# Stationary columns 16 bytes apart in place of 8, for the second weight of four of sixteen blocks

## The chip, the cores and the metric

The kernel runs on one core of a Trainium2 chip. The metric is device time in microseconds (us) of one execution. TensorE runs two kinds of instruction that matter here: a weight load (LDWEIGHTS, rows of "PEld"), which takes a stationary matrix of 128 rows and up to 128 columns from SBUF into the array, and a matmul (rows of "PE"), which streams a moving matrix of up to 512 columns through it. The load of the next matmul can run beside the matmul before it.

## The reference

```python
def _attn_ref(q, k, v):                     # q, k, v: 8 batches, 8 heads, 576 positions, 64 wide
    scores = scale * np.matmul(q, k.transpose(0, 1, 3, 2))
    bias = slopes[:, None, None] * (-np.abs(rel).astype(np.float32))[None, :, :]
    mask = (rel >= 0) & (rel < window)      # window 128
    ...                                     # softmax
    return np.matmul(attn, v).astype(np.float32)

def _moe_ref(x, w_in, w_out):               # x: 4608 tokens x 512; w_in 512x2048; w_out 2048x512
    h = np.maximum(x @ w_in, 0.0)
    return (h * h @ w_out).astype(np.float32)
```

The attention's output, one row for each token, is the input x of the two large products.

## The kernel before, in words

The 4608 tokens are worked in 9 chunks of 512 (c = 0 to 8), the 2048 hidden features in 16 blocks of 128 (f = 0 to 15). All weights are loaded once and stay in SBUF. Float32 accuracy is kept by splitting each operand in a high and a low part of the type fp32r (wh and wl of a weight, hh and hl of the hidden values) and adding three products: high by high, high by low, low by high.

For each chunk and block, `gemm1(c, f)` (matmuls in line 183) makes a 128x512 piece of the hidden layer from 4 contraction blocks of 3 products each, so 12 pairs of a weight load and a matmul; ScalarE and VectorE square and split it. `gemm2(c, f)` (matmuls in line 215) multiplies this piece by the second weight: 4 output blocks of 128 columns (m = 0 to 3), 3 products each, again 12 pairs, which add up in four PSUM banks over all f. From chunk 1 on the order on TensorE is written out in the main loop: `gemm1(n)`, `gemm2(n - 2)`, `gemm1(n + 1)`, `gemm2(n - 1)`, and so on. After every fourth `gemm1` the main loop puts the attention of a pair of heads in between: `values` of one pair (line 336) and `scores` of the next (line 388), together called a visit below. The block of `gemm2` that stands directly behind a visit has f = 1, 5, 9 or 13:

```python
                q, part = divmod(t - FIRST, 8)
```

with FIRST = 39, t = 2n or 2n + 1: part is 0 at t = 39, 47, 55, ..., so behind `gemm1` of n = 19, 23, 27, ..., and `gemm2` of n - 2 follows. Chunk 0 has an order of its own, planned ahead in `start`, in which visits of another kind stand between the blocks. Behind the last visit, in chunk 8, 35 pieces of 12 pairs follow each other without a visit.

In SBUF a weight block w[f] has for each partition two matrices (first and second weight) of 512 columns, and each column is 8 bytes: the low part and beside it the high part (the source is float64, whose two words `convert` rewrites in place). So a weight load of 128 columns reads 128 values that lie 8 bytes apart:

```python
        wh, wl = self.w[f][:, 1, :, 1], self.w[f][:, 1, :, 0]
```

Of the kernel before, what the change touches and what calls it, by code (L numbers as in the profile page):

```python
# [21 lines left out]
DM, DF = 512, 2048  # L22
NF = DF // 128
# [12 lines left out]
GO = 20  # L36
SOON = (("z", 7),)
FIRST = 39
CASTS = (0, 2, 15,)
COPIES = (3,)  # L40
SQUARES = (6,)
# [14 lines left out]
def slope(h):  # L56
    return 2.0 ** (-8.0 * (h + 1) / H)


class Kern:  # L60
# [91 lines left out]
    def weights_load(self, f):  # L152
        nc = self.nc
        at = lambda name, dt: nc.alloc_sbuf_tensor_at(f"{name}{f}", [128, 2, 512, 2], dt, offset=self.arena + f * 8192).ap()
        self.raw[f], self.w[f] = at("raw", I32), at("w", F32R)
        for i, d in enumerate((self.w1d, self.w2d.rearrange("(f p) d -> f p d", p=128))):
            nc.sync.dma_start(self.raw[f][:, i].rearrange("p d t -> p (d t)"), d[f].bitcast(I32))

    def convert(self, f):
# [8 lines left out]
        yield  # L168
        (nc.gpsimd.tensor_copy if f in CASTS else nc.scalar.copy)(wh, flo)
        yield  # L170
        nc.vector.tensor_tensor(wl, flo, wh.bitcast(F32), op=ALU.subtract)

    def gemm1(self, c, f):
        nc = self.nc
        xs = [self.x[c, p] for p in range(NP)]
        g = self.g1.tile([128, 512], F32, name="g")
        wh, wl = self.w[f][:, 0, :, 1], self.w[f][:, 0, :, 0]
        i = 0  # L180
        for cc in range(NCC):
            for w, part in ((wh, 0), (wh, 1), (wl, 0)):
                nc.tensor.matmul(  # L183
                    g, w[:, cc * 128 : cc * 128 + 128], xs[cc][:, part], start=i == 0, stop=i == 11
                )
                i += 1
                if (c, f, i) == (0, 0, 9):
                    yield
        yield
        r = self.hp.tile([128, 512], F32, name="r", bufs=1)  # L190
        hh = self.hp.tile([128, 512], F32R, name="hh")
        hl = self.hp.tile([128, 512], F32R, name="hl")
        self.h[c, f] = hh, hl
        with self.tc.high_priority(offset=100):
            nc.scalar.activation(r, g, AF.Relu)  # L195
        yield
        if c or f in SQUARES:
            nc.vector.tensor_tensor(r, r, r, op=ALU.mult)  # L198
        else:
            nc.scalar.activation(r, r, AF.Square)  # L200
        yield
        nc.scalar.copy(hh, r)  # L202
        yield
        nc.vector.tensor_tensor(hl, r, hh.bitcast(F32), op=ALU.subtract)  # L204

    def gemm2(self, c, f):
        nc = self.nc
        hh, hl = self.h.pop((c, f))
        if f == 0:
            self.acc = self.start_banks if c == 0 else [self.ac.tile([128, 512], F32, name="acc") for _ in range(4)]  # L210
        wh, wl = self.w[f][:, 1, :, 1], self.w[f][:, 1, :, 0]
        for m in range(4):
            ms = slice(m * 128, m * 128 + 128)
            for i, (w, h) in enumerate(((wh, hh), (wh, hl), (wl, hh))):
                nc.tensor.matmul(  # L215
                    self.acc[m], w[:, ms], h, start=(f == 0 and i == 0), stop=(f == NF - 1 and i == 2)
                )
            if f == NF - 1:
                o = self.op.tile([128, 512], F32, name="o")
                out = self.outd[m * 128 : m * 128 + 128, 512 * c : 512 * c + 512]  # L220
                if c == NCH - 1 and m == 3:
                    nc.scalar.copy(o[:, 0:256], self.acc[m][:, 0:256])
                    nc.vector.tensor_copy(o[:, 256:512], self.acc[m][:, 256:512])  # L223
                    nc.sync.dma_start(out[:, 0:256], o[:, 0:256])
                    nc.scalar.dma_start(out[:, 256:512], o[:, 256:512])
                    continue
                (nc.scalar.copy if m % 2 else nc.vector.tensor_copy)(o, self.acc[m])
                nc.sync.dma_start(out, o)
# [375 lines left out]
def start(K):  # L604
# [81 lines left out]
    for f in range(NF):  # L686
        d, last = CONV(f), ("w", f)
        g = K.convert(f)
        for i, (engine, us) in enumerate(CONVERT):
            if i == 3 and f in CASTS:  # L690
                engine, us = "Pool", 1.5
# [25 lines left out]
def tile_attn_moe(ctx: ExitStack, tc: tile.TileContext, *aps):  # L717
    K = Kern(ctx, tc, *aps)
    K.const()
    with tc.manual_schedule(engines={ENGINES["PE"]}):  # L720
# [4 lines left out]
        for n in range(NF, NF * NCH + 2):  # L725
            for t in (2 * n, 2 * n + 1):
                q, part = divmod(t - FIRST, 8)
                q += 9
# [17 lines left out]
def _consts():  # L746
    r = np.arange(128)
    own, h = r % 64, (r // 64)[:, None]
    cst = np.zeros((128, CST), np.float32)
    cst[:, 0:128] = np.eye(128)  # L750
    keep = own[:, None] >= np.arange(64)[None, :]
    cst[:, 128:192] = np.where(h == 0, keep, ~keep).astype(np.int32).view(np.float32)
    cst[:, 192:256] = NEG
    rel = r[:, None] - r[None, :]
    rel = np.where(rel >= 0, rel, rel + 128)
    for a in range(H):
        cst[:, 256 + 128 * a : 384 + 128 * a] = -rel * (8 * slope(a))
    later = r[:, None] < r[None, :]
    near = [cst[:, 256 + 128 * a : 384 + 128 * a] for a in range(H)]
    return np.concatenate([cst] + [np.where(late, t, np.float32(NEG)) for t in near for late in (later, ~later)], axis=1)  # L760


def _arrays(q, k, v, moe_w_in, moe_w_out):
    a = np.ascontiguousarray
    pairs = lambda x: x.transpose(1, 3, 0, 2).reshape(NP, 128, B * S)
    halo = lambda x: np.concatenate([np.zeros((NP, 128, 128), np.float32), x], axis=2)
    qt, kt = pairs(q), halo(pairs(k))
    qkd = np.stack([np.concatenate([
        qt[:, :, 512 * c : 512 * c + 256], kt[:, :, 512 * c : 512 * c + 640], qt[:, :, 512 * c + 256 : 512 * c + 512],
    ], axis=2) for c in range(NCH)])  # L770
    vt = np.zeros((NP, 1 + B * S // 128, 128, 128), np.float32)
    vt[:, 1:] = v.reshape(B, NP, 2, S, D).transpose(1, 0, 3, 2, 4).reshape(NP, B * S // 128, 128, 128)
    vd = np.stack([vt[:, 4 * c : 4 * c + 5].transpose(0, 2, 1, 3).reshape(NP, 128, 640) for c in range(NCH)])
    w1d = a(moe_w_in.reshape(NCC, 128, NF, 128).transpose(2, 1, 0, 3).reshape(NF, 128, NCC * 128))
    return [a(qkd), a(vd), w1d.view(np.int64), a(moe_w_out).view(np.int64), _consts()]


# [16 lines left out]
```

## Time and profile before

| | us |
|---|---|
| median of 3 runs | 963.27 (962.99 to 963.32) |
| time of the profiled execution | 963.21 |
| its span, first to last instruction | 961.3 |
| TensorE busy with matmuls | 953.0 (99%) |
| TensorE busy with weight loads | 790.6 (82%) |
| VectorE busy | 485.8 (51%) |
| ScalarE busy | 415.3 (43%) |
| GpSimd busy | 206.1 (21%) |

The busy time of matmuls counts each from its beginning to its modelled end; they overlap, so that the distance from one beginning to the next, and not a row's mean, says how fast they follow each other. In the chain of work that ended last, a piece such as "x12" is one `gemm1` or `gemm2`, and its length over 12 is that distance.

### The profile page before, as it was taken

Reading aid. Unit: us, or ns where it says so; the run is one execution under the profiler, and the core shown is the slowest. Engines: PE = TensorE matmul, PEld = TensorE weight load, DVE = VectorE, ACT = ScalarE, POOL = GpSimd, SP = SyncE. Lnnn points to the kernel's source line nnn. Section 1 sums busy time; section 2 is a strip of 40 time slices with the busy share of each in tenths; the row PEclk is TensorE's granted clock in tenths of the full one; section 3 lists DMA queues with packets and bytes.
Section 4 is the critical chain, followed back from the end, with each engine's and each line's share of the span. In section 5 each row is a group of like instructions: output and inputs, shape, how many; then the busy total and the mean of one; then the engine's idle time right before and its main releaser. Section 6 shows DMA issues by size and latency. Waiting matters only on the chain.

```text
span 961.3 us, 17337 instructions
## 1 busy us (share of the span) xinstructions
PE 953.0 (99%) x6392; PEld 790.6 (82%) x6392; DVE 485.8 (51%) x1335; ACT 415.3 (43%) x1107; POOL 206.1 (21%) x254
## 2 busy tenths in 40 slices
PE   9899999999999999999999999999999999999998
PEld 5688888888888888888888888888888888888886
DVE  6998864444545454544444444445445444433222
ACT  7898743333434443434443343334334343322221
POOL 4123331222222122122222222222221221120000
PEclk9999999999999999999999999999999999999999
DMA  9974423222432333222333332224332221111001
GB/s 348 404 268 151 145 72 113 83 72 64 118 83 83 83 95 105 83 67 76 118 81 83 82 109 66 81 83 127 83 83 72 66 89 42 45 44 44 1 1 44
DMA packets 73028, 95.11 MB, mean 99 GB/s; under 512 B 8048, under 2 KB 42224, under 8 KB 72944
## 3 DMA queue, kind: packets, MB, share of 16 engines
q1 hardware_dynamic: 72512, 93.49, 31.9%
q8 instruction: 50, 0.82, 0.4%
q10 hardware_dynamic: 432, 0.52, 0.2%
q14 instruction: 34, 0.28, 0.1%
HBM read 67.76 MB, written 26.21 MB: 98 GB/s over the span
## 4 chain that ended last, share of the span: by engine, by line
PE 95%; DMA 4%; ACT 0%; DVE 0%; issue 0%; SPq 0%
PE acc L215 43%; PE g L183 42%; PE at L336 6%; PE s L388 3%; PE g L388 2%; DMA raw<-in_dram 2%; DMA wide<-in_dram 1%; DMA qk<-in_dram 1%; PE at L388 0%; ACT raw L163 0%; DVE raw L165 0%; ACT t L422 0%; ACT t L415 0%; DVE o L223 0%; DVE xu L302 0%
## 5 line engine op out<-in xcount | busy, mean ns | idle before, releaser
L183 PE MATMUL g<-xu,w 128*128 128x512 f32 x1728 | 426.2, 395 | 0.8 <-issue 0.8
L183 PEld LDWEIGHTS g<-xu,w 128*128 128x128 f32 x1728 | 336.6, 195 | 66.3 <-issue 1.5
L215 PE MATMUL acc<-hh,w 128*128 128x512 f32 x1152 | 387.8, 398 | 0.0
L215 PEld LDWEIGHTS acc<-hh,w 128*128 128x128 f32 x1152 | 224.9, 195 | 45.3 <-issue 0.7
L215 PE MATMUL acc<-hl,w 128*128 128x512 f32 x576 | 227.3, 395 | 0.0
L198 DVE TENSOR_TENSOR r<-r 128x512 f32<-128x512 f32 x129 | 91.9, 712 | 263.6 <-ACT r L195 263.6
L195 ACT ACTIVATE r<-g 128x512 f32<-128x512 f32 x144 | 85.7, 595 | 314.6 <-PE g L183 311.0
L324 POOL TENSOR_SCALAR_AFFINE_SELECT pp<-pp 128x512 f32<-128x512 f32 x128 | 106.2, 830 | 242.7 <-DMA way<-pp 138.6
L204 DVE TENSOR_TENSOR hl<-r,hh 128x512 fp32r<-128x512 f32 x144 | 106.9, 743 | 68.8 <-ACT hh L202 68.3
L202 ACT CAST hh<-r 128x512 fp32r<-128x512 f32 x144 | 89.2, 620 | 109.2 <-DVE r L198 108.4
L215 PEld LDWEIGHTS acc<-hl,w 128*128 128x128 f32 x576 | 112.5, 195 | 20.5
L260 POOL TENSOR_TENSOR t<-t,nm 128x512 f32<-128x512 f32 x64 | 74.3, 1162 | 237.1 <-DVE nm L257 225.1
L249 ACT ACTIVATE t<-t,nm 128x128 f32<-128x128 f32 x256 | 99.5, 390 | 42.9 <-DVE nm L242 42.9
L434 DVE COPY_PREDICATED t<-cst,s 64x256 f32<-64x256 int32 x100 | 44.4, 444 | 41.0 <-ACT t L422 22.3
L336 PEld LDWEIGHTS at<-pp,v 128*64 128x64 f32 x1024 | 55.2, 137 | 11.4 <-issue 11.4
L336 PE MATMUL at<-pp,v 128*64 128x128 f32 x1024 | 63.0, 276 | 0.0
L242 DVE CUSTOM_DVE_ANT_0 t<-t,cst 128x128 f32<-128x128 f32 x256 | 58.5, 292 | 1.0
L311 DVE STREAM_TRANSPOSE pp<-t 128x512 f32<-128x512 f32 x64 | 45.3, 709 | 22.8 <-POOL t L260 19.9
L388 PE MATMUL s<-qk 64*64 64x64 f32 (+2 forms) x1168 | 47.5, 251 | 0.9 <-ACT raw L163 0.9
L249 ACT ACTIVATION_READ_ACCUMULATOR t<-t,nm 128x1 f32 x256 | 47.9, 187 | 0.0
L388 PEld LDWEIGHTS s<-qk 64*64 64x64 f32 x1168 | 43.0, 133 | 1.1 <-ACT raw L163 1.1
L424 POOL MEMSET t<- 64x128 f32 (+1 forms) x44 | 10.0, 228 | 146.2 <-PE g L388 137.3
(65 smaller groups left out, 476.1 us busy)
## 6 DMA issues: line engine op xcount, KB each, us to landing
raw<-in_dram SPq DMA_DIRECT2D x32, 512.0 KB, 8.7
way<-pp SPq DMA_DIRECT2D x256, 64.0 KB, 1.8
pp<-way SPq DMA_DIRECT2D x64, 256.0 KB, 2.7
qk<-in_dram SPq DMA_DIRECT2D x32, 320.0 KB, 3.7
v<-in_dram SPq DMA_DIRECT2D x32, 320.0 KB, 2.9
qk<-in_dram SPq DMA_DIRECT2D x38, 256.0 KB, 4.3
out_dram<-o SPq DMA_DIRECT2D x35, 256.0 KB, 3.0
v<-in_dram SPq DMA_DIRECT2D x3, 256.0 KB, 5.1
```

Source lines behind the costliest of these rows:

```text
L183: nc.tensor.matmul(g, w[:, cc * 128 : cc * 128 + 128], xs[cc][:, part], start=i == 0, stop=i == 11)
L195: nc.scalar.activation(r, g, AF.Relu)
L198: nc.vector.tensor_tensor(r, r, r, op=ALU.mult)
L202: nc.scalar.copy(hh, r)
L204: nc.vector.tensor_tensor(hl, r, hh.bitcast(F32), op=ALU.subtract)
L215: nc.tensor.matmul(self.acc[m], w[:, ms], h, start=(f == 0 and i == 0), stop=(f == NF - 1 and i == 2))
L242: self.nc.vector.tensor_tensor_reduce(self.t[:, m], self.t[:, m], self.K.nrel(2 * self.p + m // 2), -0.125, BIG, ALU.add, ALU.min, self.nm ...
L249: self.nc.scalar.activation(self.t[:, m], self.t[:, m], AF.Exp, bias=nm[:, m : m + 1], scale=-1.0, accum_out=nm[:, 4 + m : 5 + m],)
L260: self.nc.gpsimd.tensor_tensor(self.t, self.t, self.nm[:, 8:12].unsqueeze(2).to_broadcast([128, 4, 128]), op=ALU.mult)
L324: nc.gpsimd.affine_select(to, self.own, pattern=[[-32 * sign, 4], [0, 4], [-sign, 32]], compare_op=op, fill=0.0, base=0, channel_multiplie ...
L336: self.nc.tensor.matmul(self.X[r, o : o + 128].rearrange("p (a c) -> p a c", a=4), v[:, 2 * sg + k, r], src[:, :, 2 * j + i], start=sg == ...
L388: mm = nc.tensor.matmul(to, qk[r, q0 : q0 + 64], qk[r, k0 : k0 + 64 * n], start=True, stop=True, skip_group_check=True,)
```

## The change

In the second weight of blocks f = 1, 5, 9 and 13 the host stores the columns in another order: within each 256 columns (two output blocks of 128), a column of the one block and a column of the other stand in turn. Output block b of such a weight is then read with every second column, so its 128 values lie 16 bytes apart. All other weights are read as before, 8 bytes apart. Bytes moved, instructions and their order on every engine are the same; only the access pattern of the stationary operand differs, in 4 of 32 weight matrices, or 432 of 3456 weight loads of the two products (36 pieces of 12).

```diff
+APART = lambda i, f, b: i == 1 and f % 4 == 1
...
+    def block(self, i, f, b):
+
+        w = self.w[f][:, i]
+        if APART(i, f, b):
+            w = w.rearrange("p (n j o) t -> p n o j t", n=2, o=2)[:, b // 2, b % 2]
+        else:
+            w = w[:, 128 * b : 128 * b + 128]
+        return w[..., 0], w[..., 1]
...
-        wh, wl = self.w[f][:, 1, :, 1], self.w[f][:, 1, :, 0]
         for m in range(4):
-            ms = slice(m * 128, m * 128 + 128)
+            wl, wh = self.block(1, f, m)
             for i, (w, h) in enumerate(((wh, hh), (wh, hl), (wl, hh))):
                 nc.tensor.matmul(
-                    self.acc[m], w[:, ms], h, start=(f == 0 and i == 0), stop=(f == NF - 1 and i == 2)
+                    self.acc[m], w, h, start=(f == 0 and i == 0), stop=(f == NF - 1 and i == 2)
                 )
...
+    w2d = moe_w_out.reshape(NF, 128, DM).copy()
+    for i, w in enumerate((w1d, w2d)):
+        for f in range(NF):
+            for n in range(2):
+                if APART(i, f, 2 * n):
+                    x = w[f, :, 256 * n : 256 * n + 256]
+                    x[:] = x.reshape(128, 2, 128).transpose(0, 2, 1).reshape(128, 256).copy()
```

## Rows read from the trace of the kernel before

**Rows 1.** The page: span, busy time of TensorE, its granted clock, the chain by engine.

```profile
span 961.3 us, 17337 instructions
...
PE 953.0 (99%) x6392; PEld 790.6 (82%) x6392; DVE 485.8 (51%) x1335; ACT 415.3 (43%) x1107; POOL 206.1 (21%) x254
...
PEclk9999999999999999999999999999999999999999
...
PE 95%; DMA 4%; ACT 0%; DVE 0%; issue 0%; SPq 0%
```

**Rows 2.** The chain in order of time, window 343 to 369: start, length, what.

```profile
343.15 2.97 PE acc L215 x12
346.12 2.76 PE g L183 x12
...
365.44 1.90 PE at L336 x32
```

**Rows 3.** The same, window 549 to 575.

```profile
548.85 3.02 PE acc L215 x12
551.87 2.80 PE g L183 x12
...
571.47 1.90 PE at L336 x32
```

**Rows 4.** The chain's longest pieces over the whole span, the first and the last two behind visits.

```profile
135.84 3.00 PE acc L215 x12
...
834.76 3.02 PE acc L215 x12
859.28 3.01 PE acc L215 x12
```

**Rows 5.** The chain, window 859 to 960, behind the last visit.

```profile
862.29 2.80 PE g L183 x12
...
946.29 2.80 PE g L183 x12
```

**Rows 6.** Timeline of matmuls behind a visit: start, length, what.

```profile
368.52 0.27 PE L388 MATMUL g<-qk 64*64 64x128 f32 x1
368.72 0.51 PE L215 MATMUL acc<-hh,w 128*128 128x512 f32 x1
369.07 0.40 PE L215 MATMUL acc<-hl,w 128*128 128x512 f32 x1
369.30 0.62 PE L215 MATMUL acc<-hh,w 128*128 128x512 f32 x2
```

**Rows 7.** Timeline of weight loads at the same place.

```profile
368.72 0.19 PEld L215 LDWEIGHTS acc<-hh,w 128*128 128x128 f32 x1
368.83 0.20 PEld L215 LDWEIGHTS acc<-hl,w 128*128 128x128 f32 x1
369.07 0.43 PEld L215 LDWEIGHTS acc<-hh,w 128*128 128x128 f32 x2
```

**Rows 8.** Weight loads by line and form: count, busy us, mean ns, idle before.

```profile
L183 PEld LDWEIGHTS g<-xu,w 128*128 128x128 f32 x1728 | 336.6, 195 | 66.3 <-issue 1.5 <-ACT r L195 0.5
L215 PEld LDWEIGHTS acc<-hh,w 128*128 128x128 f32 x1152 | 224.9, 195 | 45.3 <-issue 0.7
...
L388 PEld LDWEIGHTS s<-qk 64*64 64x64 f32 x1168 | 43.0, 133 | 1.1 <-ACT raw L163 1.1
...
L503 PEld LDWEIGHTS acc<-qk__202 64*128 64x128 f32 x8 | 0.7, 186 | 0.2 <-issue 0.2
```

**Rows 9.** The page's DMA issues: the weights' transfer.

```profile
raw<-in_dram SPq DMA_DIRECT2D x32, 512.0 KB, 8.7
```

More of the change, by code (lines that the diff above doesn't have):

```diff
@@ L155, in weights_load @@
         self.raw[f], self.w[f] = at("raw", I32), at("w", F32R)
-        for i, d in enumerate((self.w1d, self.w2d.rearrange("(f p) d -> f p d", p=128))):
+        for i, d in enumerate((self.w1d, self.w2d)):
             nc.sync.dma_start(self.raw[f][:, i].rearrange("p d t -> p (d t)"), d[f].bitcast(I32))
@@ L178, in gemm1 @@
         g = self.g1.tile([128, 512], F32, name="g")
-        wh, wl = self.w[f][:, 0, :, 1], self.w[f][:, 0, :, 0]
         i = 0
         for cc in range(NCC):
+            wl, wh = self.block(0, f, cc)
             for w, part in ((wh, 0), (wh, 1), (wl, 0)):
-                nc.tensor.matmul(
-                    g, w[:, cc * 128 : cc * 128 + 128], xs[cc][:, part], start=i == 0, stop=i == 11
-                )
+                nc.tensor.matmul(g, w, xs[cc][:, part], start=i == 0, stop=i == 11)
                 i += 1
@@ L774, in _arrays @@
     w1d = a(moe_w_in.reshape(NCC, 128, NF, 128).transpose(2, 1, 0, 3).reshape(NF, 128, NCC * 128))
-    return [a(qkd), a(vd), w1d.view(np.int64), a(moe_w_out).view(np.int64), _consts()]
+    w2d = moe_w_out.reshape(NF, 128, DM).copy()
[5 more added lines that the diff above has]
+                    x[:] = x.reshape(128, 2, 128).transpose(0, 2, 1).reshape(128, 256).copy()
+    return [a(qkd), a(vd), w1d.view(np.int64), w2d.view(np.int64), _consts()]
 def kernel(**inputs):
```

## The prediction

> **What bounds the kernel now.** I read the page first. Matmuls are 95% of the chain that ended last, TensorE has a matmul under way 99% of the span, and the granted clock is full in all 40 slices, so it runs at the upper of its two levels throughout [rows 1]. No other engine and no queue can give or take much: what counts is the distance from one matmul to the next on TensorE.
>
> So next I read the chain in order of time, where one `gemm1` or `gemm2` is one piece of 12 matmuls. The reader is to see two things. First, a round from visit to visit has eight pieces: one `gemm2` directly behind the visit, 2.97 us long in the one round [rows 2] and 3.02 in another [rows 3], and seven more. Second, those seven are all alike within a round, but not from round to round: 2.76 us in the first, 2.80 in the second. Over 12 that is a spacing of 230.0 ns or 233.3 ns. I went through the 28 rounds that begin between 135.84 and 834.76 and the long stretch behind the visit before 859.28 [rows 4]: six rounds run at 230 (those from 343.15, 368.79, 394.43, 420.07, 497.35 and 678.66), one changes over midway (from 317.37), 21 run at 233. The 34 pieces behind the first of the last stretch run at 233 too [rows 5]. The line, the weights' place and the other engines' work make no difference to it: `gemm1` and `gemm2` have the same spacing, and all f. A round takes its spacing at its beginning and keeps it; I call that its gait. The block that stands at this beginning, in every round, is the one that the change touches.
>
> Last I read the loads. A load's row lasts 195 ns [rows 8], but its row is longer than the time for which it holds up the next thing. Behind a visit there is no matmul to hide the first load: the first matmul's row begins with the load, at 368.72, and the second one 0.35 us later, where the step after that is 0.23 [rows 6]. So 0.12 us of this load are seen. The second load begins 0.11 us after the first [rows 7], which says the same: the load takes its columns in for 0.11 us, and the other 0.08 of its row lie beside the matmul. From then on each load begins as the matmul before it does (both at 369.07, [rows 6, 7]), is in after 0.11 and waits for another 0.12. **A load inside a piece therefore has about 0.12 us to spare**, and only the first behind a visit is on the path.
>
> **The change, part by part.** The transfers have the same bytes and shape (32 of 512 KB, 8.7 us, [rows 9]), `convert` works on every element whatever its place, and no instruction is moved on any engine. These cost nothing, and need no cover.
>
> What is left is the price of a load with columns 16 bytes apart. The trace has none. Two rows bound it. Columns 4 bytes apart: 64 of them take 133 ns, 128 take 186 [rows 8], so 53/64 = 0.83 ns for one. Columns 8 bytes apart: 128 take 195, 9 ns more. From below: the step from 8 to 16 costs nothing, or 9 ns as the step from 4 to 8 did. From above: a column takes two places in time in place of one, 128 x 0.83 = 106 ns more; the row would then last 0.30 us, and the columns would be in after 0.22, which is just short of the 0.23 from matmul to matmul. I take the upper end, because the step from 4 to 8 shows that distance isn't free, and so that the forecast doesn't rest on a cheap load.
>
> [...]
>
> *First term: the loads seen.* 28 rounds and the last stretch begin with such a block, so 29 first loads at 0.106 us: +3.1 us (lower end: 29 x 0 = 0). The other loads of these blocks are hidden if they stay below 0.23.
>
> *Second term: the gait.* Which gait a round takes is settled within the first few matmuls behind the visit, where now the visit's end decides, and visits end variously. Afterwards twelve loads lie in between which all take twice as long and end some 10 ns ahead of the matmul that needs them, in every round alike. I expect this to even out what differs between rounds, so that they all leave the block in the same way. In which gait no row says. I choose 230: the 230 ns rounds show that 233 is not what the array needs, and a matmul held by its load until the one before is all but through begins with nothing left over from before. This is the weakest step. If it holds, each of 21 rounds saves 7 x 0.04 + 0.05 = 0.33 us [rows 2, 3]: 6.9; the round that changes midway 0.16; the last stretch 34 x 0.04 = 1.4 [rows 5]. That makes -8.4 us. Chunk 0 has some 30 pieces more at 233 (1.2 us), which I leave out of the value, since other engines' work stands between them, and take into the range.
>
> **Sum.** The profiled execution's own time is 963.21 (span 961.3 and 1.9 around it), 0.06 below the median. 963.2 + 3.1 - 8.4 = 957.9; I say **958.0**.
>
> **The rivals.**
>
> *The gait stays as it was, or turns to 233 everywhere.* The loads stay hidden and the first ones cost 3.1: 966.3 with the mix kept; with the six and a half fast rounds lost as well (6.5 x 0.33 = 2.1), 968.4. For it: 21 of 28 rounds take 233 now. Against: a block that is the same in each round takes the place of ends that vary. Chance 2 in 10. This one ends on the other side.
>
> *The load becomes the bound of its block.* If a column costs more than 0.9 ns on top (some 115 ns a load), the load is in later than the next matmul could begin, and each further ns of a load costs 36 x 11 = 396 times one ns, besides the 29 first ones. At twice the extra (212 ns, a column three times as long) the spacing in these 36 pieces goes from 233 to about 330: 396 x 0.097 + 29 x 0.212 = 38 + 6, and the time to 1000 to 1007, whatever the gait. A small excess of 10 ns with the fast gait gives 958 + 4 = 962. The same block pays if a load that lasts twice as long takes reads from the matmul beside it: 15 ns a matmul would be 396 x 0.015 = 6. For it: the upper end lies only 0.01 us under the point. Against: 106 is already a doubling. Chance 1.5 in 10.
>
> *The distance costs nothing and changes nothing.* Loads stay at 195, rounds choose as now: 963.2, give or take a few rounds of 0.33 us. For it: 4 to 8 bytes cost only 9 ns. Chance 1.5 in 10. The same cheap load with the fast gait throughout gives 963.2 - 8.4 - 1.2 = 953.6, the lowest figure here.
>
> **How the numbers follow.** My forecast, the fast gait with loads between the two ends, has 5 in 10: from 953.6 to 962. A measurement of this kernel can tell about 0.2% from no change, 1.9 us, so 961.3 to 965.2 is "the same". Faster takes nearly all of the forecast: 0.5. The same takes the case in which nothing changes, and a little of the two beside it: 0.18. Slower takes the gait at 233 with its first loads, the load as the bound, and the rest: 0.32. The range is 954 to 969: from the cheap load with the fast gait to the dear one with the slow gait; it leaves out the load as a strong bound.
>
> **What would show it.** Each step has its row: the mean of the loads of line 215 (a quarter of them at 0.30 us raises the group's mean from 195 to about 222 ns); the distance from first to second matmul behind a visit (0.35 to 0.46); the length of the seven pieces of a round (2.76 in all rounds, or not); and that of the block behind the visit (about 3.08; above 3.3 it would be bound by its loads). I am wrong if the loads are longer than 0.31 us, or if rounds at 2.80 are as frequent as before.

## The result, and the profile after

The changed kernel takes 966.33 us (median of 7 runs, 965.89 to 966.56) against 962.98 before (7 runs, 962.70 to 963.32): 1.0034 times as long, 95% interval 1.0022 to 1.0045. It is slower by 3.4 us, where 5 us less was forecast. The time lies inside the stated range, but on the other side of no change. One execution of the later run with columns 32 bytes apart took 1336 us at a granted clock of 0.655 and is left out of that run's figures.

The page of the kernel after, next to [rows 1] and [rows 8] (lines 193 and 222 are the former 183 and 215):

```profile
span 964.5 us, 17337 instructions
...
PE 956.3 (99%) x6392; PEld 810.9 (84%) x6392; DVE 485.0 (50%) x1335; ACT 415.3 (43%) x1107; POOL 206.6 (21%) x254
...
PEclk9999999999999999999999999999999999999999
...
L193 PEld LDWEIGHTS g<-xu,w 128*128 128x128 f32 x1728 | 336.9, 195 | 64.0 <-issue 1.5
L222 PEld LDWEIGHTS acc<-hh,w 128*128 128x128 f32 x1152 | 250.0, 224 | 35.3 <-issue 0.7
L222 PEld LDWEIGHTS acc<-hl,w 128*128 128x128 f32 x576 | 129.4, 225 | 15.8
```

The loads of the second weight went from a mean of 195 to 224 ns. A quarter of them changed, so one of these takes 4 x 29 = 116 ns more, about 311 (the mean of these 432 loads in the trace is 311). The granted clock has a mean of 0.999, where it was 1.000 before.

Behind a visit, timeline of matmuls and then of weight loads (compare [rows 6] and [rows 7]):

```profile
370.05 0.62 PE L222 MATMUL acc<-hh,w 128*128 128x512 f32 x1
370.52 0.40 PE L222 MATMUL acc<-hl,w 128*128 128x512 f32 x1
370.75 0.63 PE L222 MATMUL acc<-hh,w 128*128 128x512 f32 x2
```

```profile
370.05 0.31 PEld L222 LDWEIGHTS acc<-hh,w 128*128 128x128 f32 x1
370.26 0.33 PEld L222 LDWEIGHTS acc<-hl,w 128*128 128x128 f32 x1
370.52 0.55 PEld L222 LDWEIGHTS acc<-hh,w 128*128 128x128 f32 x2
```

The reader is to see the distance from the first matmul to the second: 0.47 us, and 0.35 before. The second load begins 0.21 us after the first, where it was 0.11: by the prediction's reading, that this is the time in which a load takes its columns in, that time has doubled. The next loads again begin with the matmul before them (370.52 in both).

The chain in order of time, first a round that answers to [rows 2], then the last visit and what follows it, as in [rows 4] and [rows 5]:

```profile
344.02 3.15 PE acc L222 x12
347.17 2.80 PE g L193 x12
```

```profile
863.12 3.15 PE acc L222 x12
866.26 2.80 PE g L193 x12
...
883.06 2.80 PE g L193 x12
885.87 2.83 PE acc L222 x12
888.69 2.76 PE g L193 x12
```

The block behind the visit takes 3.15 us, and the seven pieces behind it 2.80: this round has lost the gait of 230 ns that it had before. I went through all rounds: 8 of 28 now end at 2.76 (7 did before, one of them only from its middle on), 20 at 2.80. They are other rounds than before: only one round is fast in both kernels. But in the last stretch the second block with 16-byte columns, at 885.87, stands behind a running piece; it takes 2.83, and from there every piece of 8-byte loads runs at 2.76.

The sum over the trace: the 29 blocks behind visits took 146 ns more each, 4.2 us, of which 117 ns in the first matmul (29 x 0.117 = 3.4) and 29 ns in the other eleven (0.8). The other seven such blocks cost 0.2. The gait gave back 0.9 in the last stretch, 0.4 in the rounds and 0.1 in chunk 0. That is 3.0 of the 3.2 us by which the span grew.

### The profile page after: what moved, and what is told of

Same layout as the page of the kernel before. It is cut to its first block, busy times and chain, and to the rows that moved or that the text cites. A ratio compares the mean times of both kernels' runs of the same rounds, so it can differ in the third digit from the quotient of the medians.

```text
span 964.5 us, 17337 instructions
## 1 busy us (share of the span) xinstructions
PE 956.3 (99%) x6392; PEld 810.9 (84%) x6392; DVE 485.0 (50%) x1335; ACT 415.3 (43%) x1107; POOL 206.6 (21%) x254
## 4 chain that ended last, share of the span: by engine, by line
PE 97%; DVE 2%; ACT 1%; issue 0%; DVEq 0%
PE acc L222 43%; PE g L193 41%; PE at L343 6%; PE s L395 2%; PE g L395 2%; PE g L120 1%; PE s L510 0%; PE acc L510 0%; ACT tw L527 0%; DVE tw L520 0%; DVE pp L553 0%; PE at L395 0%; DVE nm L263 0%; ACT raw L164 0%; DVE xu L309 0%
## 5 line engine op out<-in xcount | busy, mean ns | idle before, releaser
L222 PEld LDWEIGHTS acc<-hh,w 128*128 128x128 f32 x1152 | 250.0, 224 | 35.3 <-issue 0.7
L222 PEld LDWEIGHTS acc<-hl,w 128*128 128x128 f32 x576 | 129.4, 225 | 15.8
```

The costliest lines, as they stand in the source:

```text
L222: nc.tensor.matmul(self.acc[m], w, h, start=(f == 0 and i == 0), stop=(f == NF - 1 and i == 2))
```

## The experiments

All were timed against the kernel before on the same chip (963.0 to 963.1 us). The gait is the spacing that the pieces of a round keep, 230 or 233 ns. Theory A: a block of 16-byte loads does set the gait of what follows, but how it leaves hangs on how it is entered: from running matmuls it leaves at 230 ns, from the empty array behind a visit it leaves either way. Theory B: these loads don't set the gait. The diffs are against the changed kernel, cut to what matters; where only the new line of APART is shown, it takes the place of the old one.

**Half of the block, the later half.**

```diff
-APART = lambda i, f, b: i == 1 and f % 4 == 1
+APART = lambda i, f, b: i == 1 and f % 4 == 1 and b >= 2
```

> Only the last two of the four output blocks (six of twelve loads) of the second weight of blocks 1, 5, 9, 13 have columns 16 bytes apart; the first load behind a visit is 8 bytes apart. Theory A (the block's gait is settled by how its 16-byte loads are entered: from a running matmul they always leave at 230 ns, from an empty array they leave either way): no exposed load, six matmuls at 235.5 ns, then 2.76 us a piece in all rounds: about 956.5 us against 963.0 before. Theory B (the loads don't settle the gait, the visit's end does): rounds stay mixed, 963 to 964 us.

Measured: 956.88 us (5 runs, 956.37 to 957.20), ratio 0.9936 (0.9923 to 0.9950). The chain of one round:

```profile
469.98 3.02 PE acc L222 x12
472.99 2.76 PE g L193 x12
475.75 2.76 PE acc L222 x12
...
489.55 2.75 PE g L193 x12
```

The last pieces run at 2.76 in 25 of 28 rounds, and in the last stretch. Theory A's time holds to 0.4 us, B is out. The three other rounds begin at 2.76 too and lose it midway; here is one, and then who waited for whom in its window 246 to 248:

```profile
241.40 2.76 PE g L193 x12
244.16 2.76 PE acc L222 x12
246.91 2.88 PE g L193 x12
249.79 2.80 PE acc L222 x12
```

```profile
PEld g L193 <- ACT r L203: 0.2, 1, 0.2
```

Here TensorE, at 2.76, reaches the bank g before ScalarE has read it, waits once, for 0.2 us, and goes on at 2.80. A fourth round of these has the wait and keeps 2.76.

**The earlier half**, the complement.

```diff
+APART = lambda i, f, b: i == 1 and f % 4 == 1 and b < 2
```

> The complement: only the first two output blocks (the first six loads) of the same weights are 16 bytes apart. Both theories: the first load behind 29 visits is exposed for 0.114 us longer, +3.3 us, and six matmuls at 235.5 ns, +0.4: about 966.5 us, with mixed gaits. If the price of the change were spread over all twelve loads in place of the first one, this would be only half of it, 964.7.

Measured: 965.13 us (10 runs, 964.82 to 965.51), ratio 1.0022 (1.0013 to 1.0031).

```profile
473.42 3.13 PE acc L222 x12
476.55 2.80 PE g L193 x12
```

In the trace the first matmul of the 29 blocks takes 117 ns longer, as in the whole change, and the other eleven 9 ns: 3.7 us. So the price is the first load's. The expectation is 1.4 us too high: it forgot that this kernel, as the changed one, gains in the last stretch and a little in the rounds (8 of 28 at 2.76), 1.4 together. Its time alone, near 964.7, would have spoken for a price spread over twelve loads; the trace's rows decide.

**The third piece in place of the first.**

```diff
+APART = lambda i, f, b: i == 1 and f % 4 == 2
```

> The 16-byte columns are moved to the second weight of blocks 2, 6, 10, 14, whose piece is the third behind a visit. Theory A: no exposed load, a piece of 2.826 us, and 2.76 us in the five pieces behind it in all rounds: 21.5 x 5 x 0.04 = 4.3 saved, 1.3 in the last stretch, 1.2 paid: about 958.6 us. Theory B: mixed gaits as before and 1.2 paid: 964.2 us.

Measured: 958.15 us (957.95 to 958.27), ratio 0.9950 (0.9938 to 0.9963).

```profile
469.90 3.00 PE acc L222 x12
472.90 2.80 PE g L193 x12
475.70 2.82 PE acc L222 x12
478.53 2.76 PE g L193 x12
```

In the round shown the gait changes from 2.80 to 2.76 behind the 16-byte piece. Of the 13 rounds that come to this piece at 2.80, 12 end at 2.76, and the other 15 keep the 2.76 that they had: 27 of 28 in all. Theory A again; the one round that stays at 2.80, from 264.08, shows no wait and is not explained.

**Half of the third piece, the earlier one.**

```diff
+APART = lambda i, f, b: i == 1 and f % 4 == 2 and b < 2
```

> Only the first six loads of the second weight of blocks 2, 6, 10, 14 (third piece behind a visit) are 16 bytes apart; six loads 8 bytes apart follow in the same piece. Theory A (what counts is that the 16-byte loads are entered from running matmuls): 2.793 us for this piece and 2.76 for the five behind it in all rounds, some 0.03 x 36 = 1.1 us less than with the whole piece: about 957.2 us. Theory G (what counts is that the 16-byte loads end a piece, as the last six did in the fast kernel and the first six did not in the slow one): rounds stay mixed, 963 to 964 us.

Measured: 958.80 us (957.79 to 959.43), ratio 0.9958 (0.9944 to 0.9972); the time is 1.6 us above the expected one, and spreads more than that of the others. The trace is of the fastest execution; why the others are slower is not shown.

```profile
473.36 2.80 PE g L193 x12
476.16 2.79 PE acc L222 x12
478.95 2.76 PE g L193 x12
```

25 of 28 rounds end at 2.76, although six loads 8 bytes apart end the piece: theory G is out. Six loads were enough when they were entered running; the same six directly behind a visit left 20 of 28 rounds at 2.80.

**The first weight**: the last half of the second piece of a round.

```diff
+APART = lambda i, f, b: i == 0 and f % 4 == 0 and b >= 2
```

> The last six loads of the first weight of blocks 0, 4, 8, 12 (second piece behind a visit) are 16 bytes apart, none of a second weight. Theory A: the piece costs at most 0.03 us more, the six pieces behind it take 2.76 us in all rounds: 21.5 x 6 x 0.04 = 5.2 saved, 1.3 in the last stretch, 0.7 paid: about 957.3 us. Theory B (the second weight's blocks behind the visit are what matters): 963 to 964 us.

Measured: 957.84 us (957.38 to 958.23), ratio 0.9947 (0.9933 to 0.9961).

```profile
470.09 3.00 PE acc L222 x12
473.09 2.82 PE g L193 x12
475.91 2.76 PE acc L222 x12
```

Which weight it is made no difference: 25 of 28 rounds end at 2.76, as with half of a second weight (`late_half`, `third_early`).

**All second weights.**

```diff
+APART = lambda i, f, b: i == 1
```

> All sixteen second weights are 16 bytes apart. Theory A: every second-weight piece 2.826 us, every first-weight piece behind it 2.76, so 5.586 for two in place of 5.600 or 5.520; exposed first loads +3.3: about 966.5 us. Theory B: second-weight pieces 2.826, first-weight pieces in the mix of before, exposed loads: about 970 us.

Measured: 967.86 us (967.79 to 968.55), ratio 1.0053 (1.0040 to 1.0066), between the two theories' times. It is 1.4 us above A's. The chain of one round shows both ways of entering in one kernel:

```profile
474.24 3.15 PE acc L222 x12
477.39 2.80 PE g L193 x12
480.19 2.83 PE acc L222 x12
483.02 2.76 PE g L193 x12
485.78 2.82 PE acc L222 x12
```

Behind the first 16-byte block, entered from the visit, the next piece takes 2.80 in 24 of 28 rounds. Behind the second one, entered running, it takes 2.76 in all 28. A's time had let every first-weight piece run at 2.76; the 24 at 2.80 are 1.0 of the 1.4 us.

**Columns 32 bytes apart**, in the place of the change, and stored in that order by the host:

```diff
-            w = w.rearrange("p (n j o) t -> p n o j t", n=2, o=2)[:, b // 2, b % 2]
+            w = w.rearrange("p (j o) t -> p o j t", o=4)[:, b]
```

> The second weights of blocks 1, 5, 9 and 13 with the columns of all four output blocks in turn, 32 bytes apart, in the place where the change has 16. Theory E (what counts is that each column needs a read of its own, so 16 and 32 bytes cost the same): loads of 309 ns, matmuls at 235.5 ns, first load seen for 0.114 us longer, 966.3 us as with the change. Theory F (the price grows with the distance, 9 ns from 4 to 8 bytes, 114 from 8 to 16): loads of 400 ns or more, these 36 pieces at 0.33 us a matmul and slower by 1.1 us each, over 1000 us.

Measured: 972.31 us (three runs, 972.01 to 972.56), ratio 1.0097 (1.0080 to 1.0114). The weight loads by line, and the chain behind a visit and in the last stretch:

```profile
L222 PEld LDWEIGHTS acc<-hh,w 128*128 128x128 f32 x1152 | 253.5, 228 | 36.3 <-issue 0.7
```

```profile
475.40 3.25 PE acc L222 x12
478.66 2.80 PE g L193 x12
...
890.13 2.93 PE acc L222 x12
893.07 2.80 PE g L193 x12
```

By this row one such load takes 4 x 33 = 132 ns more than one 8 bytes apart; the mean of all 432 in the trace is 330, where 16 bytes gave 311. Neither theory has it right, but E nearly: the large step lies between 8 and 16 bytes (+116), doubling the distance once more adds 19. Those 19 cost 9 ns in each matmul of the 36 pieces (2.93/12 = 244 ns against 235.5), 36 x 11 x 0.009 = 3.6 of the 6 us by which this run is slower than the change. Most of the rest is gait: only 3 of 28 rounds end at 2.76, where the change has 8, and in the last stretch the pieces run at 2.80 from 893.07 on. For here a block entered running leaves at 2.80, in all six that a running piece follows, so that a load which holds up its matmul was not enough to bring the fast gait.

**Columns 4 bytes apart, everywhere**, so that the sums are other ones and only the times count; in `block`, for every weight:

```diff
+        w = w.rearrange("p d t -> p (d t)")[:, 256 * b : 256 * b + 256]
+        return w[:, 0:128], w[:, 128:256]
```

> Every weight load reads 128 neighbouring words, 4 bytes apart, so low and high parts are taken in turn as if they were columns: the products are other ones, their number and sizes the same. Theory C (the reads of a load 8 bytes apart slow the matmul beside it): the spacing falls clearly below 230 ns, by 10 ns or more, and the time below 930 us. Theory D (230 or 233 is the matmul's own): spacing stays at 230 or 233, loads last 187 in place of 195 ns, first loads are seen for 8 ns less; 963 us with a mix of the two gaits, between 953 and 965.

Measured: 967.85 us (967.51 to 968.02), ratio 1.0050 (1.0034 to 1.0067). The loads by line, and a round of the chain:

```profile
L190 PEld LDWEIGHTS g<-xu,w 128*128 128x128 f32 x1728 | 324.7, 188 | 80.8 <-ACT r L200 1.2 <-issue 0.3
```

```profile
476.85 2.82 PE g L190 x12
479.66 2.81 PE acc L219 x12
482.47 2.81 PE g L190 x12
```

Loads of 188 ns, close to the 186 of [rows 8]; theory C is out, since the shorter loads brought no faster matmuls (234.3 ns). But D's time was missed too: all rounds take a third gait, 2.81 us, or 234.3 ns. The shortest loads give the slowest gait of the three.

## Why the prediction was wrong, point by point

*What bounds the kernel* held: TensorE's spacing. The granted clock was 1.00 for as long as matmuls ran and 0.50 only in the last 1.3 us of the span, and the busy times of the other engines moved by 0.8 us at most.

*The price of a load* was taken at its upper end, 106 ns, and measured 116. The intake doubled from 0.11 to 0.21 us, as "a column takes two places in time in place of one" has it. A load took 188, 195, 311 and 330 ns at 4, 8, 16 and 32 bytes, so the price doesn't grow in step with the distance: +116 ns from 8 to 16 bytes, +19 from 16 to 32. Why the large step lies between 8 and 16 bytes is not shown.

*First term, the loads seen:* forecast +3.1, measured 3.4, as 29 first matmuls by 117 ns; `early_half` against `late_half` shows that it comes with the first six loads, and the trace of `early_half` (117 ns in the first matmul, 9 in the other eleven) that it is the first of them.

*The loads inside a piece* were to be hidden by 0.01 us. They are not quite: in a piece entered running the spacing is 2.83/12 = 235.5 ns, 2 to 6 ns more than at either gait, and 244 with the longer loads of `stride32`, so these loads do hold their matmuls up. It cost 0.8 us behind visits and 0.2 elsewhere. This is the small end of the rival "the load becomes the bound".

*Second term, the gait:* this step failed. It said that twelve equal loads would make all rounds leave the block alike, and then at 230 ns, for 8.4 us. Measured: 1.4. They do not leave it alike: 20 of 28 rounds at 233 and 8 at 230, about as many as the visits alone had brought, though not the same ones. The same loads entered from running matmuls brought 230 ns, in every piece of 8-byte loads of the last stretch from 888.69 on, in 27, 25 and 25 of 28 rounds at the end of the round (`third_piece`, `third_early`, `first_weight`), and in 25 of 28 with the later half of the very block (`late_half`). So the gait can be set by such loads, as the prediction had it; the place directly behind the visit is the one at which they mostly don't bring 230, and it is also the one at which their first load is seen.

The traces show more of how a block leaves. Between the starts of its matmuls the 16-byte loads bring, after a few matmuls, three steps in turn, 235, 241 and 231 ns. Here are the ends of two blocks of the kernel after, of the one behind the visit at 344.02 and of the one entered running at 885.87, each with the start of the next piece:

```profile
346.54 0.40 PE L222 MATMUL acc<-hl,w 128*128 128x512 f32 x1
346.77 0.40 PE L222 MATMUL acc<-hh,w 128*128 128x512 f32 x1
347.01 1.09 PE L193 MATMUL g<-xu,w 128*128 128x512 f32 x4
...
888.06 0.40 PE L222 MATMUL acc<-hl,w 128*128 128x512 f32 x1
888.30 0.39 PE L222 MATMUL acc<-hh,w 128*128 128x512 f32 x1
888.53 0.85 PE L193 MATMUL g<-xu,w 128*128 128x512 f32 x3
```

In ns the last two distances are 235 and 238 in the first, which goes on at 233, and 241 and 231 in the second, which goes on at 230. I counted the blocks of the seven kernels with 16-byte columns that 8-byte loads follow, by the distance that ends at the matmul with the last 16-byte load: of the 276 where it is 240 or 241, 269 go on at 230 (mean of six distances behind), and all 63 where it is 235 go on at 233. Entered running, every such block of six or twelve loads ended on 240 or 241. Behind a visit, where the first distance is the load that is seen (some 0.46 us), 18 of the 29 blocks of the kernel after ended a step earlier, on 235 (8 on 240 or 241, 3 on 231). So the prediction's equal loads leave in unlike ways, and with each way goes the step at which the block ends. That is a regularity of these traces: no run had a number of loads that isn't a multiple of three, and so it isn't shown that the step is the cause.

The rival "the gait stays as it was", 966.3 us, is what happened, to 0.03 us, though by sums that partly cancel: 1.0 more for the inner loads, 1.4 less for the gait, 0.3 more for the first ones. Of the prediction's two signs of being wrong, rounds at 2.80 are as frequent as before (20, and 21 then), and the loads, at 311 ns, stand at the limit of 0.31 us.

*Not settled:* what in the array makes a spacing of 230, 233.3 or 234.3 ns with loads that at 8 bytes have 0.12 us to spare [rows 6, 7], and why the step at which the 16-byte loads end goes with the gait behind them. Shown is only that shorter loads brought no faster matmuls (188 ns and a spacing of 234.3 in the 4-byte run), and that loads which hold their matmuls up did not by that alone bring the fast gait (244 ns within the block and 2.80 us behind it in the 32-byte run).

## What to carry to other kernels

Look at the spacing of a long run of equal matmuls in the chain: here it had two values with a lasting gait, a perturbation of a few ns was worth 0.6% (956.88 us against 963.06), and where it was put decided its sign (966.33 against 962.98 with the whole block behind the visit). Behind a visit the second load began 0.21 us after the first with columns 16 bytes apart, and 0.11 with 8; that was all but hidden in a running piece (235.5 ns a matmul, 230 or 233 with 8 bytes) and seen in full at the first load behind a visit (+117 ns), so such loads were better put second than first (958.15 us in the third piece, 966.33 in the first). When a forecast rests on which of two states is reached, and no row says which, the forecast should stay with the states' present mix.

## What the runs showed of the hardware that was not expected

The spacing of these matmuls changed with the stride of the loads beside them, though not in its order: 234.3 ns at 4 bytes (188 ns loads), 233.3 or 230.0 at 8 (195), 235.5 at 16 (311), 244 at 32 (330). A piece at 8 bytes kept its value over up to 34 following pieces [rows 5], as a rule until a visit, a block with another stride (2.80 to 2.76 us at 885.87 in the kernel after) or a wait (0.2 us, 2.76 to 2.80 at 246.91 in `late_half`). Within a block at 16 bytes the distance went round in three steps, 235, 241 and 231 ns, and the step at which it ended went with the value that was kept behind it (240 or 241 with 230 in 269 of 276 blocks, 235 with 233 in all 63).
